# Seventeen token tiles turn their picks by a transposing DMA instead of on TensorE, with a new layout of the scattered buffer behind it

## The chip, the cores and the metric

The kernel runs on one core of one Trainium2 chip. The metric is device time in microseconds (us), from the launch of the program to its end. Five engines work side by side, each in its own fixed order: TensorE (PE; its weight loads are listed apart as PEld), VectorE (DVE), ScalarE (ACT), GpSimd (POOL) and SyncE (SP), whose only work here is to issue DMAs. An instruction whose input is not there yet holds up everything behind it on its engine.

## The reference, cut to what matters

Two layers, each a Fourier mixing followed by a product-key mixture of experts, with residuals. S = 2048 tokens, D = 512, H = 32 heads, E = 16 keys a side, 256 experts, and the best two of each side.

```
x = x + FNet(layernorm(x))        # y = Cr @ (x Wre') - Ci @ (x Wim'), C is 2048 x 2048
x = x + PEER(layernorm(x))        # and both once more, for the second layer

def PEER(x):                      # n tokens
    s1, s2 = q[..., :dk] @ k1.T, q[..., dk:] @ k2.T      # [n, 32 heads, 16] each
    i1, i2 = top 2 of s1, top 2 of s2                    # places, and values t1, t2
    cand   = t1[..., :, None] + t2[..., None, :]         # four sums of a head
    top_s, top_e = best 2 of cand, with e = 16 * i1 + i2
    g   = softmax(top_s)                                 # two weights of a head
    act = gelu(x @ u[top_e])
    out = sum over heads and picks of g * act * v[top_e]
```

## The kernel before

**Tiling.** The 2048 tokens are 16 tiles of 128. Each layer runs nine sequence units in the order `ORDER`: layer 0 takes units 0 to 8, layer 1 takes 0, 7, 1, 2, 3, 4, 5, 6, 8. Units 0 to 6 are 256 tokens (two tiles each), units 7 and 8 one tile each (tiles 14 and 15). The place of a unit in that order is called `at`. In a unit, `seq_unit` multiplies the whole layer-normed input (`xh` and `xl`, the high and low parts of fp32) with a block of the sequence DFT matrix. A block comes by DMA (`raw`, L454, four buffers), ACT takes its high part (`ch`, L458), DVE its low part (`cl`, L462), three buffers each, and PE runs three 128x512 matmuls for each of 64 pairs (L518). Then `ptl` and `pth` hold the result's parts (L544, L547).

**A token tile.** `token_tile` follows for each tile of the unit: the second DFT (L668), residual and layernorm (L682), the scores of all heads and keys (`pc`, L784 and L788), the scores of all experts (`xu`, L818), a long series of DVE steps that finds the best picks, and the matrix `q` of 3 x 128 columns a token (first place, second place and weight; each 2 x 2 x 32), written last by L985 and L1007. From there:

- PE turns `q` with three f16 transposes of 128x128 (`f_pq`, L1018), ACT copies the result out of PSUM (`f_qt`, L1022) as `qt`, with the heads' places reordered.
- DVE compares `qt` with a ramp into one-hot masks (`lr`, L1041, four a tile) and puts the weights on two of them (L1047, two a tile): "the masks".
- PE multiplies the masks in 32 small matmuls (L1057): "the blocks", two banks `pg`.
- ACT copies them to SBUF (L1089), two DMAs scatter them to DRAM (`gdr`, L1116), two read them back by token (`gt`, L1124), DVE multiplies them with the gelu (L1131), and either PE turns the product (L1162) and multiplies it with `v` (L1181, L1185), or, for the layer-1 tiles of `DEFERRED`, the product is stored (`ptd`, L1153) and multiplied at the end (`off`, L597).

**What sets the order.** All this is recorded as `Op`s with a duration, what they come after, which buffers (`Hold`) they take and give back, and a priority. `Plan.run` lays them out in time by these numbers, and the program is issued in the order of the planned starts. `lag` is the planned time from a DMA's issue to its landing, `shy` a further margin that its readers get, and `wary` a margin of 0.8 us (`WARY`) that PE operations of the middle stage get after inputs of other engines. Nothing of the plan waits at run time: an engine waits only for the semaphores of the data. The pools `q` (two buffers), `qt` (one), `lr` (four) and the eight lanes of DMAs in flight (`LANES`) bound what can overlap.

**Other moved work.** `MOVED` tiles (25 of 32) already turn their layernormed input over DRAM (`xdr`, L726; `tok`, L735, four DMAs) after a DVE transpose of 32x32 blocks, instead of on PE (L754).

Of the kernel before, what the change touches and what calls it, by code (L numbers as in the profile page):

```python
# [8 lines left out]
F32 = mybir.dt.float32  # L9
# [7 lines left out]
P = 128  # L17
# [7 lines left out]
SP = 1  # L25
# [15 lines left out]
    return at >= 2 if layer == 0 else at < NCH + NSC * (TPC - 1) - 2  # L41


def DEFERRED(layer, at):
    return layer == 1 and at < NCH + NSC * (TPC - 1) - 2


LATE = 13
STEP = 5 * E
ROW = 16 * STEP - E  # L50
WARY = 0.8
FILL0 = 10
FIRST = 4
# [14 lines left out]
class Op:  # L68
    def __init__(self, n, engine, us, fn, after, take, last, prio, lag, behind, shy):
        self.shy = shy  # L70
        self.n, self.engine, self.us, self.fn, self.prio, self.lag = n, engine, us, fn, prio, lag
        self.after, self.take, self.last, self.behind = after, take, last, behind
        self.start = self.end = None
        middle = len(prio) >= 4 and prio[0] == 0 and 3 <= NCH * prio[1] + prio[2] < 2 * NCH - 2 and prio[2] >= 0
        self.wary = WARY if engine == "PE" and middle else 0.0


# [85 lines left out]
def act(n):  # L163
    return 0.09 + n / 1.2e3
# [7 lines left out]
def spectral_peer_kernel(ctx: ExitStack, tc, x_in, cseq, ctile, dhid, wq, k1t, k2t, ut, vm, out):  # L172
# [7 lines left out]


    BUFS = {"acc": 4, "bank": 4, "raw": 4, "c": 3, "p": 1, "row": 4, "wr": 5, "wp": 2,
            "tok": 3, "sc": 1, "eq": 1, "act": 3, "q": 2, "top": 1, "qt": 1, "lr": 4, "gt": 1, "pp": 1, "gdr": 2, "xdr": 2, "bn": 1, "pick": 1}
    plan = Plan(BUFS)


# [423 lines left out]
    def token_tile(layer, n, i, t0, at):  # L610
# [408 lines left out]

        def f_qt():  # L1020
            t["qt"] = piece((3, P), dtype=F16) if fine else work([P, 3, P], F16, "qt")
            nc.scalar.copy(t["qt"].rearrange("p r (q j) -> p r q j", q=16),  # L1022
                           t["pq"].rearrange("p r (j q) -> p r q j", q=16))

        a = op("PE", 3 * TR16 + 0.06, f_pq, [c5, d2], take=[hb], last=[hq], prio=prio)
        a_qt = op("ACT", act(384), f_qt, [a], take=[hqt], last=[hb], prio=prio)

        def row_of(r, hf):
            m = t["qt"][:, r].rearrange("p (a b) -> p a b", b=4)[:, 16 * hf:16 * hf + 16]
# [22 lines left out]
        def f_blocks(hfs=(0, 1)):  # L1052
            for hf in hfs:
                pg = t["pg", hf] = bank([P, 8, E, 4])
                for g in range(8):
                    for j in range(2):
                        nc.tensor.matmul(pg[j * 64:(j + 1) * 64, g], t["m", hf, 0][:, 2 * g + j],  # L1057
                                         t["m", hf, 1][:, 2 * g + j], start=True, stop=True)

        def f_mask():  # L1060

# [48 lines left out]
        for hf in range(0 if fine else 2):  # L1110
            def f_out(hf=hf):
                if hf == 0:
                    t["gdr"] = dram.tile([2, E, 4, ROW], F32, name="gdr", bufs=BUFS["gdr"])
                d = t["gdr"][0]
                d = bass.AP(d.tensor, d.offset + hf * 8 * STEP, [[ROW, P], [STEP, 8], [1, 4 * E]])
                nc.sync.dma_start(d, t["gs", hf].rearrange("p g t e -> p g (t e)"))  # L1116
            moves.append(op("SP", 0.6, f_out, evac[hf:hf + 1], behind=moves[-1:], take=[] if hf else [hd], last=[hgs[hf]], prio=prio, lag=2.7))
        for j in range(0 if fine else 2):
            def f_in(j=j):
                if j == 0:  # L1120
                    t["gt"] = work([P, E, E], F32, "gt")
                d = t["gdr"][j]
                d = bass.AP(d.tensor, d.offset, [[STEP, 64], [4 * ROW, E], [1, E]])
                nc.sync.dma_start(t["gt"][j * 64:(j + 1) * 64], d)  # L1124
            back.append(op("SP", 0.6, f_in, moves, behind=back, take=[] if j else [hgt], last=[hd], prio=prio, lag=3.2, shy=0.5))
        if fine:
# [218 lines left out]
```

## Time and profile before

| what | value |
|---|---|
| median of 3 runs | 1234.31 us (1233.75 to 1234.34) |
| the profiled execution, its own time | 1233.48 us |
| its span in the trace | 1231.7 us |
| PE busy | 1220.1 us, 99% |
| DVE busy | 1000.1 us, 81% |
| ACT busy | 492.2 us, 40% |
| POOL busy | 45.0 us, 4% |
| DMA queue of SP, share of the 16 engines | 48.2% |
| granted TensorE clock | 1.00 |

Times are counted from the start of the span. Matmuls overlap in PE's pipeline: a 128x512 one is listed with some 0.39 us but the next starts about 0.23 us after it. What an instruction costs PE is therefore read from the starts of its neighbours, not from its own duration. Layer 0 fills roughly 7 to 660 us of the span (the preparation of the weights runs in its first 190 us, beside units 0 and on), layer 1 the rest. The page's columns are: line, engine, operation, output and inputs by the program's names, busy time, mean, and idle time before it with what ended it.

### The profile page before, as it was taken

How to read it: one execution, taken by the hardware profiler on the slowest of the kernel's cores; microseconds unless marked ns; L12 is line 12 of the kernel's file. 1: busy time of each engine (PE TensorE's matmuls, PEld its weight loads, DVE VectorE, ACT ScalarE, POOL GpSimd, SP SyncE). 2: the span in 40 equal slices, each digit the busy share in tenths (PEclk: the TensorE clock that was granted, in tenths of full speed). 3: DMA queues.
4: the chain of work that ended last, by engine and by line, in shares of the span. 5: the costliest groups of instructions: out<-in, count | busy, mean ns of one | idle time of the engine just before them, and what ended most of it. 6: DMA issues, size and time to landing. Idle time of an engine off the chain costs nothing. (4 is left out here: it accounts for less than half of the span.)

```text
span 1231.7 us, 20733 instructions
## 1 busy us (share of the span) xinstructions
PE 1220.1 (99%) x7626; PEld 1014.5 (82%) x7626; DVE 1000.1 (81%) x2272; ACT 492.2 (40%) x1010; POOL 45.0 (4%) x71
## 2 busy tenths in 40 slices
PE   9999999999999999999999999999999999999998
PEld 6877778878788888899988988788888888888886
DVE  8899997999897785968987359959596786859796
ACT  7522234334343333324654233334343333343455
POOL 2000000000000000000000000000000000000000
PEclk9999999999999999999999999999999999999999
DMA  7866551453444244441656243563635254454464
GB/s 241 261 200 218 188 169 35 101 119 83 123 122 113 70 116 116 107 120 49 172 142 174 79 120 82 125 135 92 154 97 140 73 145 111 99 141 104 115 204 144
DMA packets 312726, 160.12 MB, mean 130 GB/s; under 512 B 216752, under 2 KB 283056, under 8 KB 312624
## 3 DMA queue, kind: packets, MB, share of 16 engines
q1 hardware_dynamic: 312480, 158.66, 48.2%
q8 instruction: 60, 0.98, 0.3%
q14 instruction: 42, 0.34, 0.1%
q10 hardware_dynamic: 144, 0.13, 0.0%
HBM read 120.73 MB, written 38.01 MB: 129 GB/s over the span
## 5 line engine op out<-in xcount | busy, mean ns | idle before, releaser
L518 PE MATMUL acc<-ch,xh 128*128 128x512 f32 (+1 forms) x868 | 328.3, 378 | 0.8 <-DVE ptl L547 0.8
L518 PE MATMUL acc<-cl,xh 128*128 128x512 f32 (+1 forms) x868 | 321.9, 371 | 0.0
L518 PE MATMUL acc<-ch,xl 128*128 128x512 f32 (+1 forms) x868 | 321.7, 371 | 0.0
L458 ACT CAST ch<-raw 128x512 fp32r<-128x512 f32 x256 | 158.6, 620 | 272.0 <-PE acc L518 222.7
L462 DVE TENSOR_TENSOR cl<-raw,ch 128x512 fp32r<-128x512 f32 x256 | 176.0, 688 | 61.6 <-ACT ch L458 51.4
L518 PEld LDWEIGHTS acc<-cl,xh 128*128 128x128 f32 x868 | 163.6, 188 | 28.8
L518 PEld LDWEIGHTS acc<-ch,xh 128*128 128x128 f32 x868 | 163.6, 189 | 28.0 <-issue 1.8
L518 PEld LDWEIGHTS acc<-ch,xl 128*128 128x128 f32 x868 | 163.8, 189 | 25.6
L880 DVE TENSOR_TENSOR tmp<-sc 128x512 f32<-128x512 f32 (+1 forms) x64 | 43.5, 680 | 72.9 <-ACT sc L793 72.6
L784 PE MATMUL bank<-wh,tok 128*128 128x512 f32 x256 | 100.3, 392 | 0.3 <-ACT tok L742 0.3
L784 PE MATMUL bank<-wl,tok 128*128 128x512 f32 x256 | 99.7, 389 | 0.0
L668 PE MATMUL bank<-dh,pth 128*128 128x512 f32 x248 | 98.6, 397 | 0.0
L668 PE MATMUL bank<-dl,pth 128*128 128x512 f32 x248 | 96.7, 390 | 0.0
L668 PE MATMUL bank<-dh,ptl 128*128 128x512 f32 x248 | 93.6, 390 | 0.0
L793 ACT COPY sc<-bank 128x512 f32<-128x512 f32 x62 | 36.1, 588 | 138.1 <-PE bank L788 108.0
L1041 DVE TENSOR_TENSOR lr<-iota,qt 128x1024 f16<-128x1024 f16 x124 | 81.0, 686 | 12.0 <-ACT qt L1022 11.9
L260 POOL TENSOR_TENSOR stats<-stats,half 128x1 f32<-128x1 f32 x64 | 43.7, 689 | 1149.1 <-DVE stats L257 1135.1
L867 DVE TENSOR_TENSOR eq<-sc,val 128x1024 f16<-128x1024 f32 (+1 forms) x64 | 77.2, 1207 | 1.5
L518 PE MATMUL acc<-ch,xg 128*128 128x512 f32 (+1 forms) x204 | 77.3, 379 | 0.0
L518 PE MATMUL acc<-cl,xg 128*128 128x512 f32 (+1 forms) x204 | 75.7, 371 | 0.0
L518 PE MATMUL acc<-ch,xm 128*128 128x512 f32 (+1 forms) x204 | 75.7, 371 | 0.0
L788 PE MATMUL bank<-wh,tok 128*128 128x512 f32 x256 | 68.4, 389 | 0.0
(190 smaller groups left out, 2057.8 us busy)
## 6 DMA issues: line engine op xcount, KB each, us to landing
raw<-in_cseq SPq DMA_DIRECT2D x224, 256.0 KB, 2.8
wr<-in_wq SPq DMA_DIRECT2D x32, 512.0 KB, 3.8
gdr<-lr SPq DMA_DIRECT2D x62, 256.0 KB, 3.7
raw<-in_ctile SPq DMA_DIRECT2D x32, 256.0 KB, 2.9
xdr<-lr SPq DMA_DIRECT2D x25, 256.0 KB, 2.8
tok<-xdr SPq DMA_DIRECT2D x100, 64.0 KB, 2.6
wr<-in_x SPq DMA_DIRECT2D x16, 256.0 KB, 3.3
row<-in_x SPq DMA_DIRECT2D x16, 256.0 KB, 4.0
```

Of the source, the lines that this page charges most:

```text
L260: nc.gpsimd.tensor_tensor(st[:, 1:2], st[:, 1:2], half, op=ALU.pow)
L458: nc.scalar.copy(t[1], t[0])
L462: nc.vector.tensor_sub(t[2], t[0], as32(t[1]))
L518: nc.tensor.matmul(target(d), w[s][:, d * P:(d + 1) * P], moving(s % per, part), start=(s == 0 and k == 0 and d % blocks == 0), stop=(s == ...
L668: nc.tensor.matmul(t["y", cs.start], w[:, k, c, t0:t0 + P], r[:, c, k, cs], start=(not fine and z == 0 and c == 0 and m == 0), stop=(z == ...
L784: nc.tensor.matmul(t["pc", hf], t["th"][:, k, :], r[:, k, hf], start=(k == 0 and r is wh), stop=False)
L788: nc.tensor.matmul(t["pc", hf], t["tl"][:, k, :], wh[:, k, hf], start=False, stop=(k == KD - 1))
L793: nc.scalar.copy(t["sc"][:, :, hf, :], t["pc", hf].rearrange("p h e -> p e h"))
L867: nc.vector.tensor_tensor(t["eq"][:, :, cols], scores(), val(rank_, cols), op=ALU.is_equal)
L880: nc.vector.tensor_max(t["tmp"][:, :, cols], flat("sc")[:, :8, cols], flat("sc")[:, 8:, cols])
L1041: nc.vector.tensor_tensor(t["m", hf, r], io2, row_of(r, hf), op=ALU.is_equal)
```

## The change

`Q_MOVED` names 17 tiles: in layer 0 the places 2 to 4 (units 2, 3 and 4: tiles 4 to 9), in layer 1 the places 1 to 6 (units 7, 1, 2, 3, 4 and 5: tile 14 and tiles 2 to 11). For them the three transposes on PE and the copy on ACT are gone. SP stores `q` to DRAM (`qdr`, new line L1036) and loads it back with one transposing DMA of 384 x 128 f16 (L1040). The plan reckons 0.45 us and a lag of 2.0 us for the first, 1.2 us, a lag of 2.5 us and a margin (`shy`) of 2.0 us for the second. `qt` gets a second buffer.

[...] Last, `wary` begins at place 1 of layer 0 instead of place 3.

```
+def Q_MOVED(layer, at):
+    return ((2 <= at < 5) if layer == 0 else (1 <= at < 7))
-STEP = 5 * E
-ROW = 16 * STEP - E
+ROW = 68 * E
-        middle = len(prio) >= 4 and prio[0] == 0 and 3 <= NCH * prio[1] + prio[2] < 2 * NCH - 2 and prio[2] >= 0
+        middle = len(prio) >= 4 and prio[0] == 0 and 1 <= NCH * prio[1] + prio[2] < 2 * NCH - 2 and prio[2] >= 0
-    BUFS = {... "qt": 1, ...}
+    BUFS = {... "qt": 2, ... "qdr": 2, ...}
...
         def f_qt():
             t["qt"] = piece((3, P), dtype=F16) if fine else work([P, 3, P], F16, "qt")
-            nc.scalar.copy(t["qt"].rearrange("p r (q j) -> p r q j", q=16),
-                           t["pq"].rearrange("p r (j q) -> p r q j", q=16))
-        a = op("PE", 3 * TR16 + 0.06, f_pq, [c5, d2], take=[hb], last=[hq], prio=prio)
-        a_qt = op("ACT", act(384), f_qt, [a], take=[hqt], last=[hb], prio=prio)
+            if fine:
+                nc.scalar.copy(t["qt"].rearrange("p r (q j) -> p r q j", q=16),
+                               t["pq"].rearrange("p r (j q) -> p r q j", q=16))
+            else:
+                nc.scalar.copy(t["qt"], t["pq"])
+
+        if Q_MOVED(layer, at):
+            hqd = Hold("qdr")
+            def f_out():
+                t["qdr"] = dram.tile([3, P, P], F16, name="qdr", bufs=BUFS["qdr"])
+                nc.sync.dma_start(t["qdr"].rearrange("r t c -> t r c"), t["q"].rearrange("p r k a h -> p r (k a h)"))
+            def f_in():
+                t["qt"] = work([P, 3, P], F16, "qt")
+                nc.sync.dma_start(t["qt"].rearrange("p r t -> p (r t)"), t["qdr"].rearrange("r t c -> (r t) c"), transpose=True)
+            a = op("SP", 0.45, f_out, [c5, d2], take=[hqd], last=[hq], prio=prio, lag=2.0)
+            a_qt = op("SP", 1.2, f_in, [a], take=[hqt], last=[hqd], prio=prio, lag=2.5, shy=2.0)
+        else:
+            a = op("PE", 3 * TR16 + 0.06, f_pq, [c5, d2], take=[hb], last=[hq], prio=prio)
+            a_qt = op("ACT", act(384), f_qt, [a], take=[hqt], last=[hb], prio=prio)
...
-                        nc.tensor.matmul(pg[j * 64:(j + 1) * 64, g], t["m", hf, 0][:, 2 * g + j],
-                                         t["m", hf, 1][:, 2 * g + j], start=True, stop=True)
+                        half, n = (hf, 2 * g + j) if fine else (j, 8 * hf + g)
+                        nc.tensor.matmul(pg[j * 64:(j + 1) * 64, g], t["m", half, 0][:, n], t["m", half, 1][:, n], start=True, stop=True)
...
-                    t["gdr"] = dram.tile([2, E, 4, ROW], F32, name="gdr", bufs=BUFS["gdr"])
-                d = t["gdr"][0]
-                d = bass.AP(d.tensor, d.offset + hf * 8 * STEP, [[ROW, P], [STEP, 8], [1, 4 * E]])
+                    t["gdr"] = dram.tile([3 * E * 4 + 4, ROW], F32, name="gdr", bufs=BUFS["gdr"])
+                d = t["gdr"]
+                d = bass.AP(d.tensor, d.offset + hf * 32 * (ROW + E), [[ROW, P], [4 * (ROW + E), 8], [1, 4 * E]])
-            moves.append(op("SP", 0.6, f_out, ..., lag=2.7))
+            moves.append(op("SP", 0.6, f_out, ..., lag=3.1))
...
-                d = t["gdr"][j]
-                d = bass.AP(d.tensor, d.offset, [[STEP, 64], [4 * ROW, E], [1, E]])
+                d = t["gdr"]
+                d = bass.AP(d.tensor, d.offset + j * 64 * ROW, [[ROW + E, 64], [4 * ROW, E], [1, E]])
```

Since the plan is laid out anew, the order moves on every engine. Below it is shown for one moved tile, tile 9 of layer 0 (the second tile of unit 4, `at` 4). The line numbers of the changed program are 3 to 21 higher than those of the program before: L668 becomes L671, L547 L550, L462 L465, L985 and L1007 L988 and L1010, L1041 L1061, L1047 L1067, L1057 L1078, L1131 L1151.

On PE before, among the second DFT's matmuls of the same unit (`bank_5463`), the three transposes of tile 9's `q_5207` with their weight loads:

```order
L668 MATMUL bank_5463<-dh_100,pth_5386 128x512
L668 MATMUL bank_5463<-dl_101,pth_5386 128x512
L668 MATMUL bank_5463<-dh_100,ptl_5387 128x512
L1018 LDWEIGHTS q_5207
L1018 MATMUL bank_5473<-ident16_109,q_5207 128x128
L1018 LDWEIGHTS q_5207
L1018 MATMUL bank_5473<-ident16_109,q_5207 128x128
L1018 LDWEIGHTS q_5207
L1018 MATMUL bank_5473<-ident16_109,q_5207 128x128
L668 MATMUL bank_5463<-dh_100,pth_5386 128x512
L668 MATMUL bank_5463<-dl_101,pth_5386 128x512
L668 MATMUL bank_5463<-dh_100,ptl_5387 128x512
```

On PE now, the same unit's second DFT; tile 9's `q` is read nowhere on this engine:

```order
L671 MATMUL bank_5399<-dh_100,pth_5332 128x512
L671 MATMUL bank_5399<-dl_101,pth_5332 128x512
L671 MATMUL bank_5399<-dh_100,ptl_5333 128x512
L521 MATMUL acc_4751<-ch_5289,xg_83 128x512
L521 MATMUL acc_4751<-ch_5289,xm_99 128x512
L521 MATMUL acc_4751<-cl_5300,xg_83 128x512
```

Over the whole program 51 transposes and 51 weight loads are gone from PE, and nothing is added there.

On DVE before, tile 9 again: its last two writes of `q_5207`, one row of another tile, and the masks that read `qt_5483`:

```order
L985 TENSOR_TENSOR q_5207<-key_5208,df_5448 128x2x64
L1007 TENSOR_TENSOR q_5207<-gw_5454,q_5207 128x2x32
L1170 TENSOR_TENSOR pp_5470<-bank_5460,pp_5470 128x256
L1041 TENSOR_TENSOR lr_5485<-iota_110,qt_5483 128x1024
L1041 TENSOR_TENSOR lr_5487<-iota_110,qt_5483 128x1024
L1041 TENSOR_TENSOR lr_5496<-iota_110,qt_5483 128x1024
L1047 TENSOR_TENSOR lr_5487<-lr_5487,qt_5483 128x1024
```

On DVE now (`q_5198` and `qt_5447` are the same tile's):

```order
L988 TENSOR_TENSOR q_5198<-key_5199,df_5418 128x2x64
L1010 TENSOR_TENSOR q_5198<-gw_5420,q_5198 128x2x32
L550 TENSOR_TENSOR ptl_5333<-acc_4751,pth_5332 128x512
L465 TENSOR_TENSOR cl_5465<-raw_5257,ch_5456 128x512
L465 TENSOR_TENSOR cl_5470<-raw_5278,ch_5459 128x512
L550 TENSOR_TENSOR ptl_5333<-acc_4763,pth_5332 128x512
L1151 TENSOR_TENSOR act_5005<-act_5005,gt_5435 128x256
L1061 TENSOR_TENSOR lr_5492<-iota_110,qt_5447 128x1024
L1061 TENSOR_TENSOR lr_5505<-iota_110,qt_5447 128x1024
L1190 TENSOR_TENSOR pp_5503<-bank_5494,pp_5503 128x256
L1067 TENSOR_TENSOR lr_5505<-lr_5505,qt_5447 128x1024
```

Five rows of other work now stand between the last write of `q` and the first mask, where one stood; over the 17 tiles it is 5 to 20 rows now and 0 to 7 before.

On SP before, the queue in the same stretch; no DMA of `q` is in it:

```order
L1228 DMA x2d_120<-row_4591 128x512
L454 DMA raw_5528<-in_cseq 128x2x256
L1116 DMA gdr_5581<-lr_5579 128x8x64
L1116 DMA gdr_5581<-lr_5583 128x8x64
L1124 DMA gt_5616<-gdr_5581 64x16x16 x2
L454 DMA raw_5630<-in_cseq 128x2x256
```

On SP now (`gdr_5387` and `gt_5435` are tile 8's, one tile before):

```order
L1136 DMA gdr_5387<-lr_5376 128x8x64
L1136 DMA gdr_5387<-lr_5389 128x8x64
L1036 DMA qdr_5433<-q_5198 128x3x128
L1144 DMA gt_5435<-gdr_5387 64x16x16 x2
L1040 DMA_TRANSPOSE qt_5447<-qdr_5433 128x384
L457 DMA raw_5468<-in_cseq 128x2x256
L457 DMA raw_5483<-in_cseq 128x2x256
L1248 DMA x2d_120<-row_4422 128x512
```

The store of `q` and the transposing load stand on either side of tile 8's reading back, and two loads of the DFT matrix stand behind them.

More of the change, by code (lines that the diff above doesn't have):

```diff
@@ L182, in spectral_peer_kernel @@
     BUFS = {"acc": 4, "bank": 4, "raw": 4, "c": 3, "p": 1, "row": 4, "wr": 5, "wp": 2,
-            "tok": 3, "sc": 1, "eq": 1, "act": 3, "q": 2, "top": 1, "qt": 1, "lr": 4, "gt": 1, "pp": 1, "gdr": 2, "xdr": 2, "bn": 1, "pick": 1}
+            "tok": 3, "sc": 1, "eq": 1, "act": 3, "q": 2, "top": 1, "qt": 2, "lr": 4, "gt": 1, "pp": 1, "gdr": 2, "xdr": 2, "qdr": 2, "bn": 1, "pick": 1}
     plan = Plan(BUFS)
@@ L1112, in f_out @@
                 if hf == 0:
-                    t["gdr"] = dram.tile([2, E, 4, ROW], F32, name="gdr", bufs=BUFS["gdr"])
-                d = t["gdr"][0]
-                d = bass.AP(d.tensor, d.offset + hf * 8 * STEP, [[ROW, P], [STEP, 8], [1, 4 * E]])
+                    t["gdr"] = dram.tile([3 * E * 4 + 4, ROW], F32, name="gdr", bufs=BUFS["gdr"])
+                d = t["gdr"]
+                d = bass.AP(d.tensor, d.offset + hf * 32 * (ROW + E), [[ROW, P], [4 * (ROW + E), 8], [1, 4 * E]])
                 nc.sync.dma_start(d, t["gs", hf].rearrange("p g t e -> p g (t e)"))
-            moves.append(op("SP", 0.6, f_out, evac[hf:hf + 1], behind=moves[-1:], take=[] if hf else [hd], last=[hgs[hf]], prio=prio, lag=2.7))
+            moves.append(op("SP", 0.6, f_out, evac[hf:hf + 1], behind=moves[-1:], take=[] if hf else [hd], last=[hgs[hf]], prio=prio, lag=3.1))
         for j in range(0 if fine else 2):
```

## The prediction

> **What bounds the kernel now.** I read the page's busy lines first, then the stages, then PE alone row by row. The page:
>
> ```profile
> span 1231.7 us, 20733 instructions
> PE 1220.1 (99%) x7626; PEld 1014.5 (82%) x7626; DVE 1000.1 (81%) x2272; ACT 492.2 (40%) x1010; POOL 45.0 (4%) x71
> ```
>
> PE is the bound, and DVE has a fifth of the span to spare. The stages (length, then busy time of PE, PEld, DVE, ACT, POOL) show where PE still idles:
>
> ```profile
> 190.00:300.00 110.00, 108.66 (x640) 89.19 (x639) 100.96 (x252) 43.08 (x98) 3.81 (x5) 1.00 0.38 88
> 300.00:470.00 170.00, 169.12 (x953) 138.28 (x952) 140.94 (x344) 62.33 (x133) 8.51 (x12) 1.00 0.42 106
> 835.00:1145.00 310.00, 310.00 (x1693) 255.40 (x1692) 238.29 (x560) 117.02 (x247) 4.85 (x9) 1.00 0.47 116
> 1145.00:1232.00 87.00, 82.00 (x671) 71.44 (x669) 68.40 (x182) 45.60 (x103) 1.10 (x2) 0.99 0.55 160
> ```
>
> Between 835 and 1145 us, where ten of the seventeen changed tiles lie, PE idles 0.00 us: every slot taken off PE there shortens the run, and every wait put on PE lengthens it. The granted clock (third column from the end) is 1.00, and 0.99 in the last stage, so the clock takes no part.
>
> **The transposes (a gain).** What three of them cost PE is read from the starts of their neighbours. First the regular step, from the chain, then PE's timeline at the first and the last changed tile:
>
> ```profile
> 815.36 1.81 PE bank L784 x8
> ...
> 302.17 0.34 PE L1018 MATMUL bank<-ident,q 128*128 128x128 f16 x3
> 302.32 0.47 PE L518 MATMUL acc<-ch,xh 128*128 128x512 f32 x1
> 302.64 0.39 PE L518 MATMUL acc<-ch,xl 128*128 128x512 f32 x1
> ...
> 1142.58 0.34 PE L1018 MATMUL bank<-ident,q 128*128 128x128 f16 x3
> 1142.73 0.48 PE L668 MATMUL bank<-dh,pth 128*128 128x512 f32 x1
> 1143.04 0.39 PE L668 MATMUL bank<-dl,pth 128*128 128x512 f32 x1
> ```
>
> Eight matmuls in 1.81 us make a step of 0.227 us. The three transposes hold PE for 0.15 us (302.17 to 302.32), but the matmul behind them then takes 0.32 us until its successor starts, 0.09 more than a step. So the triple costs 302.64 - 302.17 - 0.227 = 0.24 us, and at 1142.58 as much. The same difference, taken at all 17 (with 0.12 us for the step where a 128x256 matmul follows), has a median of 0.245 us and a sum of 4.17 us. Nothing comes to PE in their stead (51 matmuls fewer, none more), and the blocks stay. Term: -4.17 us. By its busy time (mean 0.22 us each) the gain would look like 11 us; that counts the pipeline three times.
>
> [...]
>
> **ACT, PSUM, plain copy (nothing).** 17 copies of `qt` leave ACT, which is busy 40%, and the 14 plain copies that stay can only change there. 17 short holds of a PSUM bank go; where PE idles 0.00 us, a bank that comes free earlier buys nothing. Zero.
>
> **The margin `wary` from place 1 on (a gain).** Three stalls of PE lie in the two places that become wary (tile 2 twice, tile 4 once):
>
> ```profile
> 252.00 0.39 PE L518 MATMUL acc<-cl,xh 128*128 128x512 f32 x1
> 252.73 0.34 PE L1018 MATMUL bank<-ident,q 128*128 128x128 f16 x3 [0.35 <-DVE q L985]
> ...
> 272.34 0.39 PE L518 MATMUL acc<-cl,xg 128*128 128x512 f32 x1
> 273.03 0.44 PE L1162 MATMUL bank<-identf,act 128*128 128x128 f32 x2 [0.30 <-DVE act L1131]
> ...
> 321.44 0.39 PE L518 MATMUL acc<-cl,xh 128*128 128x512 f32 x1
> 322.70 0.44 PE L1162 MATMUL bank<-identf,act 128*128 128x128 f32 x2 [0.88 <-DVE act L1131]
> ```
>
> Start to start less one step, they cost 0.50, 0.46 and 1.03 us. A margin of 0.8 us takes the first two and 0.8 of the third: 1.76 us. The new order agrees: counted in steps, PE has 0.7 us more work ahead of tile 2's transposes, and between blocks and L1162 2.7 us more for tile 2 and 2.1 for tile 4. Bounds 0 (the plan slips elsewhere) and 1.99 (all three); I take 1.76.
>
> **The way over DRAM (a possible loss).** Of such a transposing load the trace has no row. Its way is: last write of `q`, store, load, first mask. The nearest DMAs (count, KB each, median us from issue to landing):
>
> ```profile
> x2d<-row SPq DMA_DIRECT2D x16, 256.0 KB, 2.0
> gdr<-lr SPq DMA_DIRECT2D x62, 256.0 KB, 3.7
> tok<-xdr SPq DMA_DIRECT2D x100, 64.0 KB, 2.6
> wr<-in_dhid SPq DMA_DIRECT2D x4, 512.0 KB, 4.5
> gt<-gdr SPq DMA_DIRECT2D x62, 64.0 KB, 3.0
> ```
>
> The store (96 KB in pieces of 256 bytes) lies between 2.0 and 3.7 us; the load (96 KB) between 2.6 and 4.5 us, if a transposing one is like some plain one. Together 4.6 to 8.2 us; I take 6.5, above the middle, since the pieces are small as in `gdr`, and since for tile 9 the load stands behind tile 8's reading back, which itself waits for `gdr` (3.7 us).
>
> What the order allows is read for tile 9, one of the two tightest. Before, on DVE and PE:
>
> ```profile
> 450.19 0.23 DVE L1007 TENSOR_TENSOR q<-gw,q 128x64 f16<-128x64 f32 x1 [0.37 <-ACT q L1006]
> ...
> 452.32 1.90 DVE L1041 TENSOR_TENSOR lr<-iota,qt 128x1024 f16<-128x1024 f16 x3 [1.26 <-ACT qt L1022]
> ...
> 456.54 0.67 DVE L1047 TENSOR_TENSOR lr<-lr,qt 128x1024 f16<-128x1024 f16 x1
> ...
> 458.64 0.69 PE L1057 MATMUL bank<-lr 128*64 128x64 f16 x32
> ```
>
> From the last write of `q` (450.42) to the first mask took 1.90 us, and the masks were done (457.21) 1.43 us ahead of the blocks, of which 0.4 us is the least that this hop took in any changed tile (tile 5). From tile 9's scores to its blocks the order now has 18 more matmuls and six transposes fewer: 18 x 0.227 - 6 x 0.05 = 3.8 us more of PE's work. So the way may take 1.9 + 3.8 + 1.0 = 6.7 us before PE waits. The same working gives 6.7 us for tile 11 of layer 1, 7.6 for its tile 5, 8.2 for its tile 10, and 9.4 to 22 us for twelve others. Only for tile 5 of layer 0 it gives nothing, since its blocks moved up 3.2 us: there other DVE work left the way (20 rows stand between `q` and masks now). At 6.5 us no tile waits; at 8.2 us three do, by 1.5, 1.5 and 0.6: 3.6 us. Bounds 0 and 3.6; I take 0.5, as some tile will be late.
>
> **The SP queue.** The load waits there for the store's landing, up to 3.7 us, with loads of the DFT matrix (`raw`) behind it. Those have cover (who waited for what: us in total, times, longest):
>
> ```profile
> SPq L454 <- DVE cl L462: 320.4, 129, 15.0
> ...
> ACT ch L458 <- DMA raw<-in_cseq: 5.7, 4, 2.7
> ...
> DVE act L1131 <- DMA gt<-gdr: 1.9, 2, 1.3
> ```
>
> SP spends 320 us waiting for a free `raw` buffer, and ACT waits only 5.7 us in all for one to land. Four buffers at one block in 12 steps (2.7 us) are 10.9 us ahead. 34 DMAs of 96 KB add 3.3 MB to 160. Zero; if the cover were gone, a late `ch` would be next. SP's issue itself has no row and no reader beside these.
>
> **The layout of `gdr`.** Number and size of the pieces stay, the distances change; what that does to 3.7 and 3.0 us no row shows. It lies between a few tenths less and, taking the 4.5 us row as the worst, 0.8 + 1.5 us more. Before, DVE waited for `gt` twice in all, 1.9 us (last row above), so most of it is hidden; and in PE's order the work between blocks and L1162 is 1.3 to 2.7 us more than before for tiles 1 to 5, and from 1.4 less to 2.0 more for the rest of layer 0. Zero, with the upper end in the range.
>
> **The end.** After 1155 us the chain runs through DVE for some 30 us, starting behind the scores of the last pair of tiles:
>
> ```profile
> 1154.71 0.60 ACT sc L793
> ```
>
> Those scores come earlier as PE does, so the gain passes on, unless tile 11's masks, 2.4 us later against PE's work, push this DVE stretch: bounds 0 and +2.4, taken 0, since its blocks stand ahead of that stretch.
>
> **The sum**, against the profiled execution (1233.48 us, span 1231.7): -4.17 - 1.76 + 0.5 = -5.43, so 1228.05. That execution was 0.83 us below the median 1234.31; on the median's footing 1228.9 us.
>
> **Rivals.**
>
> A. *Only the transposes pay, and a part is given back at the end.* The new order stalls PE in other places as much as the three stalls did (term 0 instead of -1.76), and tile 11 pushes the DVE stretch by 2.4 us: 1234.31 - 4.17 + 2.4 = 1232.5, within 0.2%. For it: the end is already DVE's. Against: the transposes alone make 1230.1, and the margin acts just where the stalls are.
>
> B. *The masks come late and PE waits (slower).* If the way takes longer than the order allows, DVE stands at the mask with `cl` behind it, PE at the blocks, and each changed tile pays anew. At 9.3 us tile 9 pays 2.6, tile 11 2.6, tile 5 of layer 1 1.7 and tile 10 1.1: 8.0 us, so 1228.4 (no 0.5) + 8.0 = 1236.4; about there it turns from no change to slower (over 1236.8). At 12 us ten tiles pay 27 us, and the time passes 1250. For it: the transposing load is the one operation here without a row. Against: 9.3 us is 1.1 above the worst pair of plain DMAs.
> [...]
>
> C. *Loads of `raw` fall behind the waiting SP.* One late `ch` costs up to the 2.7 us seen; two or three such make 1234 to 1236, no change. Against: the waits quoted above.
>
> **How the numbers follow.** About 0.2% (2.5 us) is what a measurement of this kernel tells from no change. The forecast has 0.60, and milder forms of A that still end below 1231.8 have 0.04: faster 0.64. A has 0.12 and C 0.07: no change 0.19. B has 0.17: slower. The time is the forecast's, 1228.9. Low end: 1234.31 - 4.17 - 1.99 = 1228.1, and 0.8 for small waits that a new order may also take away, 1227.3. High end: 1237.0, just past B's turning point; beyond it lies somewhat over 0.1.
>
> **What would show it.** PE's matmuls 7575 instead of 7626, its busy time some 4 us lower, and idle time in 190 to 300 us down from 1.34 us towards 0.5. The transposing load's landing: below 4.5 us confirms the way, above 6 brings B. A wait of DVE's mask for `qt<-qdr` with several us in all, and of PE's blocks behind it, would be B's mark; ACT's `ch` waiting for `raw` well over 5.7 us C's; and 835 to 1145 us is where any such wait shows as idle PE. A load that lands late, or takes all 16 DMA engines for long, would make the prediction wrong.

## The result, and the profile after

The changed kernel takes 1226.32 us (median of 6 runs, 1225.76 to 1227.04), the one before 1234.32 us (1233.69 to 1234.88). The ratio is 0.9936, with a 95% interval of 0.9923 to 0.9948: 8.0 us less. Forecast were 5.4 us less, and 1226.32 lies 1 us below the low end of the range, 1227.3. The profiled execution of the changed kernel took 1226.32 us too, with a span of 1224.5 us; the one of before had 1233.48 and 1231.7. So 7.2 of the 8.0 us can be looked for in the two traces, and the remaining 0.8 us is that the profiled execution of before lay below its median.

Page of the changed kernel:

```profile
span 1224.5 us, 20672 instructions
PE 1216.2 (99%) x7575; PEld 1013.4 (83%) x7575; DVE 999.3 (82%) x2272; ACT 483.0 (39%) x993; POOL 48.9 (4%) x71
```

7575 matmuls and 3.9 us less of busy PE, as foreseen. The stages of the changed kernel (length, then busy time of PE, PEld, DVE, ACT and POOL, granted clock, DMA share, GB/s):

```profile
190.00:300.00 110.00, 110.00 (x642) 90.46 (x642) 99.29 (x247) 41.81 (x96) 3.64 (x5) 1.00 0.34 87
300.00:470.00 170.00, 170.00 (x953) 140.31 (x952) 141.10 (x350) 60.68 (x131) 10.62 (x12) 1.00 0.47 118
835.00:1145.00 310.00, 309.88 (x1670) 255.84 (x1669) 236.65 (x545) 110.18 (x228) 6.17 (x10) 1.00 0.48 121
1145.00:1232.00 87.00, 74.84 (x636) 65.40 (x634) 63.30 (x170) 44.23 (x100) 0.55 (x1) 0.98 0.55 159
```

In the first two stages PE idled 1.34 and 0.88 us before; now it idles 0.00 in both. Between 835 and 1145 us, where ten tiles go over DRAM, 0.12 us of idle time has come. The last row counts 7.2 us less of PE because the run ends that much earlier. The transfers of the changed kernel (count, KB each, median us from issue to landing):

```profile
gdr<-lr SPq DMA_DIRECT2D x62, 256.0 KB, 2.9
tok<-xdr SPq DMA_DIRECT2D x100, 64.0 KB, 2.6
gt<-gdr SPq DMA_DIRECT2D x62, 64.0 KB, 3.0
qdr<-q SPq DMA_DIRECT2D x17, 96.0 KB, 1.8
qt<-qdr SPq DMA_TRANSPOSE x17, 2.4
```

The store of `q` lands after 1.8 us and the transposing load after 2.4 us. Both are below the lower bounds that the rows of before gave (2.0 and 2.6). What the one tile shown in the prediction makes of it, tile 9 of layer 0, on DVE, SP and PE of the changed kernel:

```profile
443.13 0.23 DVE L1010 TENSOR_TENSOR q<-gw,q 128x64 f16<-128x64 f32 x1
443.38 0.38 SPq L1036 DMA_DIRECT2D qdr<-q  x1
445.26 1.28 SPq L1040 DMA_TRANSPOSE qt<-qdr  x1
449.40 1.28 DVE L1061 TENSOR_TENSOR lr<-iota,qt 128x1024 f16<-128x1024 f16 x2
...
454.85 0.68 DVE L1067 TENSOR_TENSOR lr<-lr,qt 128x1024 f16<-128x1024 f16 x1
...
457.11 0.69 PE L1078 MATMUL bank<-lr 128*64 128x64 f16 x32
```

The last write of `q` ends at 443.36; SP issues the load (445.26) once the store has landed, 1.8 us after its issue, and its landing is recorded at 448.2. That makes a way of 4.85 us. DVE is at other work then and comes to the masks 1.2 us later; the masks are done 1.6 us ahead of the blocks. In all 17 tiles the way has a median of 4.7 us, 4.1 to 4.9 us in fourteen of them and 8.1 us in the slowest (tile 14 of layer 1, whose store stood 2 us in SP's queue and took 3.7 us to land). The waits of the changed kernel (who waited for what: us in total, times, longest):

```profile
ACT tok L745 <- DMA tok<-xdr: 7.2, 5, 2.1
ACT ch L461 <- DMA raw<-in_cseq: 5.6, 3, 2.1
...
DVE act L1151 <- DMA gt<-gdr: 4.7, 2, 4.3
...
DVE lr L1061 <- DMA qt<-qdr: 1.4, 1, 1.4
```

Of 17 tiles one mask waited for its load, 1.4 us (the slow one). ACT's wait for `raw` is as it was. What grew is ACT's wait for `tok`, from 1.4 to 7.2 us, and DVE's for `gt`, from 1.9 to 4.7.

**Where the 7.2 us are.** I took every matmul's start-to-start time less the step of its form (0.227 us for 128x512 and so on; own working over all of PE's rows). What is left over falls into the short groups with the slower matmul behind them, and into stalls of over 0.13 us:

| us | before | after | difference |
|---|---|---|---|
| triples of `q` and the slower matmul behind each | 7.68 | 4.00 | -3.68 |
| stalls 190 to 590 us | 2.88 | 0.00 | -2.88 |
| stalls 590 to 670 us | 0.49 | 0.87 | +0.38 |
| stalls 670 to 1145 us | 0.99 | 0.75 | -0.24 |
| stalls from 1145 us on | 1.50 | 0.89 | -0.61 |
| everything else | | | -0.14 |
| span | 1231.71 | 1224.54 | -7.17 |

So the triples brought about half, and the stalls 3.35 us, where the prediction had 1.76 - 0.5 = 1.26. 2.88 of the stalls went between 190 and 590 us; the three named ones are 1.99 of that. The fourth was at the blocks of tile 0. PE before:

```profile
219.82 0.44 PE L1057 MATMUL bank<-lr 128*64 128x64 f16 x16
220.95 0.44 PE L1057 MATMUL bank<-lr 128*64 128x64 f16 x16 [0.69 <-ACT lr L1089]
```

And PE after, the same blocks:

```profile
219.31 0.69 PE L1078 MATMUL bank<-lr 128*64 128x64 f16 x32
```

The second sixteen of the 32 blocks waited for ACT's copy of the first sixteen: in the program before, both halves of tile 0 lie in the same PSUM bank, and in no other tile do they. After the change they have two, and all 32 run in one go. This is worth 0.86 us (start to start), and it was not in my sum. Which banks the halves get changes with other edits of the program too: in the kernel with the new layout alone (below), whose order is that of before, they have two. So this gain is an accident of the new program and not the work of the moves.

### The profile page after: what moved, and what is told of

Read it like the earlier page. It is cut to its first block, busy times and chain, and to the rows that moved or that the text cites. A ratio compares the mean times of both kernels' runs of the same rounds, so it can differ in the third digit from the quotient of the medians.

```text
span 1224.5 us, 20672 instructions
## 1 busy us (share of the span) xinstructions
PE 1216.2 (99%) x7575; PEld 1013.4 (83%) x7575; DVE 999.3 (82%) x2272; ACT 483.0 (39%) x993; POOL 48.9 (4%) x71
## 4 chain that ended last, share of the span: by engine, by line
PE 93%; DVE 4%; DMA 1%; SPq 0%; ACT 0%; issue 0%; POOL 0%; ACTq 0%; DVEq 0%; POOLq 0%
PE acc L521 52%; PE bank L671 12%; PE bank L787 9%; PE bank L791 5%; PE bank L821 3%; PE bank L521 2%; PE bank L1078 2%; PE acc L600 2%; PE bank L1201 1%; PE bank L395 1%; DVE w L387 1%; DVE w L384 1%; PE bank L1205 1%; PE acc L501 1%; PE acc L671 1%; DMA wr<-in_wq 1%
## 5 line engine op out<-in xcount | busy, mean ns | idle before, releaser
L465 DVE TENSOR_TENSOR cl<-raw,ch 128x512 fp32r<-128x512 f32 x256 | 175.3, 686 | 60.6 <-ACT ch L461 44.9
L671 PE MATMUL bank<-dh,pth 128*128 128x512 f32 x248 | 98.0, 395 | 0.5 <-ACT pth L547 0.5
L671 PE MATMUL bank<-dl,pth 128*128 128x512 f32 x248 | 96.6, 390 | 0.0
L671 PE MATMUL bank<-dh,ptl 128*128 128x512 f32 x248 | 93.6, 391 | 0.0
L263 POOL TENSOR_TENSOR stats<-stats,half 128x1 f32<-128x1 f32 x64 | 47.6, 748 | 1138.3 <-DVE stats L260 1064.8
L1061 DVE TENSOR_TENSOR lr<-iota,qt 128x1024 f16<-128x1024 f16 x124 | 80.7, 683 | 2.1 <-DMA qt<-qdr 1.4
```

The lines of the kernel that those rows point to most:

```text
L263: nc.gpsimd.tensor_tensor(st[:, 1:2], st[:, 1:2], half, op=ALU.pow)
L465: nc.vector.tensor_sub(t[2], t[0], as32(t[1]))
L671: nc.tensor.matmul(t["y", cs.start], w[:, k, c, t0:t0 + P], r[:, c, k, cs], start=(not fine and z == 0 and c == 0 and m == 0), stop=(z == ...
L1061: nc.vector.tensor_tensor(t["m", hf, r], io2, row_of(r, hf), op=ALU.is_equal)
```

## Experiments

Each of them is compared with the kernel before, run on the same chip; its medians there were 1234.1 to 1234.2 us. "Stalls" are the stalls of PE after 190 us, by the working above; before has 5.86 us of them, after 2.51. Where the text says "triples", the slower matmul behind each is counted with them.

**The new layout of `gdr` alone** (the kernel before, with the plain copy, the new pairing of the blocks and the new distances; the order of instructions is the same on every engine). The plain copy leaves the heads' places in `qt` as they are in `q`, as the transposing load does, so the blocks pair other columns of the masks and their results stand elsewhere in `gdr`. There are still two stores of 8 pieces of 256 bytes a partition, with the rows of neighbouring partitions 4352 bytes apart instead of 5056, and two loads of 16 pieces of 64 bytes a token, with neighbouring tokens 4416 bytes apart instead of 320.

```
-STEP = 5 * E
-ROW = 16 * STEP - E
+ROW = 68 * E
...
+                        half, n = (hf, 2 * g + j) if fine else (j, 8 * hf + g)
...
+                d = bass.AP(d.tensor, d.offset + hf * 32 * (ROW + E), [[ROW, P], [4 * (ROW + E), 8], [1, 4 * E]])
```

> The kernel before with the new layout of gdr alone (plain copy of qt, other pairing of the masks, other distances); the planned numbers and so the order of every engine stay as before. In the result the stores of gdr landed after 2.9 us instead of 3.7. Theory S (the gain is PE's slots, 17 x 0.245 us, and the stalls that the margin wary takes away): the layout pays nothing by itself, 1234.3 within 0.5 us, and the stalls of PE at L1162 (0.46 us for tile 2, 1.03 us for tile 4) stay. Theory L (the faster stores took the stalls away): gt is read 0.8 us earlier, both stalls go, 1.3 us less, 1233.0.

Measured: 1232.47 us (1231.84 to 1232.97), ratio 0.9986 (0.9977 to 0.9995). The scattered store lands after 3.0 us instead of 3.7, but the stalls that wait for its reading back stayed as long as they were. PE of this kernel:

```profile
272.16 0.44 PE L1164 MATMUL bank<-identf,act 128*128 128x128 f32 x2 [0.30 <-DVE act L1133]
...
321.81 0.44 PE L1164 MATMUL bank<-identf,act 128*128 128x128 f32 x2 [0.85 <-DVE act L1133]
```

0.30 and 0.88 us before, 0.30 and 0.85 now. So the faster store takes none of the three stalls away. Laid beside before, matmul by matmul, the profiled execution gains 0.86 us at tile 0's blocks, which here have two banks, and 0.29 us at 602 us, and little more until the end (1.2 us in all). The median fell by 1.8 us where no change was expected: 0.86 us of that is the banks, and the rest is not traced to a cause. Nothing that waits for the stores or their reading back got shorter by more than 0.03 us at the two stalls, so zero for the layout's own transfers stands.

**The margin alone** (the kernel before with one line):

```
-        middle = ... and 3 <= NCH * prio[1] + prio[2] < 2 * NCH - 2 and prio[2] >= 0
+        middle = ... and 1 <= NCH * prio[1] + prio[2] < 2 * NCH - 2 and prio[2] >= 0
```

> The kernel before with wary from place 1 of layer 0 on, nothing else. Theory S: the three stalls of tiles 2 and 4 go (1.76 us), 1232.5. Theory L: only the one at tile 2's transposes, which no store stands before, goes: 0.5 us, 1233.8. Theory P (any new plan draws its stalls anew, by chance): between 1232 and 1236, with other stalls in other places.

Measured: 1232.27 us (1231.36 to 1233.79), ratio 0.9986 (0.9977 to 0.9994). The three stalls are gone, and tile 0's too, but a new one of 0.93 us has come in the same stretch, PE of this kernel:

```profile
380.21 0.34 PE L1018 MATMUL bank<-ident,q 128*128 128x128 f16 x3 [0.76 <-DVE stats L257]
```

and 0.57 us near the end. Stalls are 4.63 us, 1.23 less than in before, although the three and tile 0's bank were 2.85: the margin does what it says where it says it, and more than half of the sum comes back elsewhere. The 1.97 us less of the median agree with theory S's 1.76 in part by accident, since tile 0's bank is in them and the new stalls are too.

**The moved tiles without the margin** (the changed kernel with that line put back):

> The changed kernel with wary from place 3 again. Theory S: the stalls at places 1 and 2 come back, up to 1.8 us, 1228.1. Theory L: 1226.3 to 1226.8, the faster stores still cover them. Theory P: 1225 to 1230, with stalls in new places.

Measured: 1230.06 us (1229.24 to 1230.30), ratio 0.9966 (0.9953 to 0.9978). Triples 3.84 us, near the changed kernel's 4.00. Stalls are 5.58 us. Of the three that the margin was to take, only the first is back, smaller (0.35 us start to start), and the largest stall is new; PE of this kernel:

```profile
251.72 0.34 PE L1021 MATMUL bank<-ident,q 128*128 128x128 f16 x3 [0.19 <-DVE q L988]
...
600.39 0.50 PE L671 MATMUL bank<-dh,pth 128*128 128x512 f32 x1 [1.84 <-ACT pth L547]
```

The row at 600.39 is the second DFT waiting for its input, in a place with no moved tile; it costs 2.0 of the 5.58 us. Theory S gave 1228.1 with all three stalls back; two stayed away without the margin. So the new order can take them as well as the margin can, and which of the two took them in the changed kernel is not separated.

**The margin and the layout without the moves** (the changed kernel with `Q_MOVED` returning False):

> The changed kernel with no tile moved (the layout, the margin wary, the lag of 3.1 us and two buffers of qt stay): the 17 triples are back on PE. Theory S: 17 x 0.245 = 4.2 us more than the changed kernel, 1230.5, and the profile's triples sum to 32 again. Theory P: anywhere from 1229 to 1234, by the stalls of its plan.

Measured: 1230.55 us (1230.33 to 1231.02), ratio 0.9971 (0.9960 to 0.9982), as expected. From here to the changed kernel the 17 moves bring 4.2 us. Triples 7.56 against 4.00 us: 3.6 us, or 0.21 us each. The two traces differ by 4.7 us, and the rest is that this plan has 1.1 us more of stalls; so the 4.2 us agree with 17 x 0.245 in part by luck. Between 190 and 590 us this kernel has 1.03 us of stalls, the margin alone 0.93: the planned landing of 3.1 us and the second buffer of `qt`, which both stay here, do not empty that stretch either.

**What a transpose costs PE** (the kernel before, with every triple but the last tile's done twice, 93 transposes more):

```
-            for r in range(3):
+            for r in [0, 1, 2] * (1 if fine else 2):
```

> The kernel before, with the three transposes of q issued twice in a row in every tile but the last (31 tiles, 93 more matmuls of the same data into the same bank); the order is otherwise as before, and the plan doesn't know of them. Theory S (0.056 us a step inside a group, 0.09 us once for the change back to fp32 matmuls): 93 x 0.056 = 5.2 us more, less the 0.9 us that tile 0's blocks waited in the kernel before and don't in this program (their two banks lie apart): 1238.5. Rival G (a triple costs 0.245 us wherever it stands): 31 x 0.245 - 0.9 = 6.7 us more, 1240. Rival R (the busy time of 0.22 us a transpose is what it costs): 20 us more, 1254.

Measured: 1237.96 us (1235.97 to 1239.88), ratio 1.0030 (1.0018 to 1.0042). PE of this kernel:

```profile
302.06 0.51 PE L1018 MATMUL bank<-ident,q 128*128 128x128 f16 x6
302.37 0.48 PE L518 MATMUL acc<-ch,xh 128*128 128x512 f32 x1
302.69 0.40 PE L518 MATMUL acc<-ch,xl 128*128 128x512 f32 x1
```

Six hold PE 0.31 us (three held it 0.15), and the matmul behind them takes 0.32 us until its successor, as behind three. Over all of them the 93 more cost 5.36 us, 0.058 each, and the slower matmul behind costs the same as before, about 0.09 a group. So the price read from the starts, 0.15 + 0.09 a triple, is the right one, and neither the busy time (0.22 us each) nor the same price per triple wherever it stands (rival G, 1240 us) is. What the 0.09 us come from is not shown. It is not the change from f16 back to fp32 that theory S named, since the matmul behind a pair of fp32 transposes is as slow. PE of the kernel before:

```profile
322.89 0.47 PE L518 MATMUL acc<-ch,xh 128*128 128x512 f32 x1
323.21 0.39 PE L518 MATMUL acc<-ch,xl 128*128 128x512 f32 x1
```

These stand behind the two transposes L1162 at 322.70 us and step 0.32 us; behind all 19 such pairs that a 128x512 matmul follows the median is 0.314 us, as behind the 27 triples that one follows.

**A longer way** (the changed kernel, with `q` copied twice from DRAM to DRAM between store and load; the plan does not know of it):

```
+                for n in range(2):
+                    far = dram.tile([3, P, P], F16, name=f"far{n}", bufs=BUFS["qdr"])
+                    nc.sync.dma_start(far, t["qdr"])
+                    t["qdr"] = far
```

> The changed kernel with the way over DRAM made longer: q goes through two more DRAM buffers (two copies of 96 KB, each waiting for the one before) ahead of the transposing load; the planned order stays. In the changed kernel's trace the way took 4.1 to 4.9 us in 14 of 17 tiles and the first mask began 1.2 to 6.5 us after the landing in all tiles but one. Theory W (PE pays what the way exceeds the order's allowance): some 4.4 us more of way, paid by six or so tiles with 9 us in all, 1235. Rival H (the allowance is far larger or refilled elsewhere): 1226.5. Rival Q (SP stands longer in its queue, the DFT blocks come late): well over 1240, with ACT waiting for raw.

Measured: 1249.11 us (1247.51 to 1251.09), ratio 1.0122 (1.0108 to 1.0135); the way is 8.7 to 13.0 us. Waits of this kernel:

```profile
DVE lr L1065 <- DMA qt<-far: 21.1, 12, 6.2
ACT tok L745 <- DMA tok<-xdr: 20.7, 7, 6.0
PE bank L1082 <- DVE lr L1071: 10.7, 6, 3.0
...
ACT ch L461 <- DMA raw<-in_cseq: 6.0, 4, 2.3
```

Twelve masks wait, and PE behind them, while `raw` is no later than before. This is rival B with the mechanism that it named, but both prices were too low: the expectation by some 14 us, and rival B's working, which gave 8 us for a way of 9.3 us, the median here. Stalls are 26.6 us, 24.1 more than in the changed kernel. A part is told by PE's timeline behind one of these waits:

```profile
813.76 1.02 PE L1082 MATMUL bank<-lr 128*64 128x64 f16 x31 [2.96 <-DVE lr L1071]
...
816.16 0.63 PE L521 MATMUL acc<-ch,xh 128*128 128x512 f32 x1
816.58 0.63 PE L521 MATMUL acc<-ch,xl 128*128 128x512 f32 x1
```

and by the stretches around it, of the same kernel (columns as in the stages above, granted clock third from the end):

```profile
810.00:813.70 3.70, 0.68 (x2) 0.40 (x3) 3.11 (x6) 0.62 (x1) 0.00 (x0) 0.90 0.72 207
813.70:820.00 6.30, 6.24 (x44) 5.08 (x44) 1.30 (x3) 1.60 (x3) 0.00 (x0) 0.52 0.92 232
820.00:826.00 6.00, 6.00 (x34) 5.16 (x33) 1.11 (x2) 1.50 (x3) 0.00 (x0) 1.00 0.52 67
```

After the wait the matmuls step 0.427 us instead of 0.227 for some 5 us; the granted clock of the stretch from 813.70 to 820 us is 0.52. There are 33 such steps after 190 us in this kernel (one in before, one in the changed kernel), 6.6 of the 24.1 us. The other 17.5 us are waits, 10.7 of them blocks waiting for late masks (the third row above). How the rest divides is not separated: SP also has the two copies in its queue, which land after 2.3 and 2.2 us, and ACT waits 20.7 us for `tok` against 7.2 in the changed kernel.

**No margin for the load's landing** (the changed kernel, `shy=0.0` for the transposing load in place of 2.0):

> The changed kernel with the margin (shy) of the transposing load at 0 instead of 2.0 us: masks are planned up to 2 us earlier. Theory S (the margin is not what the gain rests on; the plan without it still reckons 6.2 us for a way of some 4.5): 1226.3 within 1 us. Rival M (the margin keeps PE from waiting): 1228 to 1231, with waits of DVE for qt<-qdr of several us. Theory P (a new plan draws new stalls): up to 2 us either way without such waits.

Measured: 1230.33 us (1229.47 to 1231.50), ratio 0.9969 (0.9956 to 0.9981). The masks hardly wait for the load, as the waits of this kernel show:

```profile
DVE lr L1061 <- DMA qt<-qdr: 1.0, 2, 0.7
```

Yet stalls are 7.26 us, 3.09 of them between 590 and 670 us, where no tile is moved; of the moved tiles' blocks only those of tile 14 of layer 1 waited for their masks, 0.56 us. So most of the 4.0 us lost are not waits for the load. The time is rival M's, its mechanism (several us of masks waiting) is not there; new stalls of a new plan, as in theory P, are, though twice as large as it allowed.

**Twenty-five tiles** (the changed kernel with more tiles moved):

```
-    return ((2 <= at < 5) if layer == 0 else (1 <= at < 7))
+    return ((1 <= at < 7) if layer == 0 else (at < 7))
```

> The changed kernel with 25 tiles moved instead of 17 (layer 0 places 1 to 6, layer 1 places 0 to 6). Theory S: eight more triples off PE, 8 x 0.245 = 2.0 us less, 1224.3. Theory P: the new plan's stalls add or take up to 2 us. Rival B: the tiles at the layer's edges are needed soon, PE waits there, 1227 to 1230.

Measured: 1229.90 us (1229.82 to 1231.60), ratio 0.9967 (0.9954 to 0.9979). The triples fall further, to 2.41 us with a wait of 0.5 us inside one group, but stalls rise to 9.0 us, 4.0 of them between 590 and 670 us, and ACT waits 14.4 us for `tok`:

```profile
ACT tok L745 <- DMA tok<-xdr: 14.4, 6, 3.7
```

So eight triples more bring no gain: the time is rival B's (1227 to 1230), 3.6 us above the changed kernel. Between 190 and 590 us this kernel has 1.7 us of stalls, although it has the moves and both margins.

**Plans a little beside it.** By then the triples were settled and the stalls were not: every new order had others. So four kernels that differ from before or after in one number of the plan alone, in no computation: the load's margin 1.7 and 2.3 in place of 2.0, the margin `WARY` 1.0 in place of 0.8, and the kernel before with 2.8 for 2.7 us of landing in the store of `gdr`.

```
-... hqd], prio=prio, lag=2.5, shy=2.0)      # after
+... hqd], prio=prio, lag=2.5, shy=1.7)      # and, in another kernel, shy=2.3
...
-WARY = 0.8                                  # after
+WARY = 1.0
...
-... last=[hgs[hf]], prio=prio, lag=2.7))    # before
+... last=[hgs[hf]], prio=prio, lag=2.8))
```

> The changed kernel with a margin of 1.7 us instead of 2.0 on the transposing load, a small nudge of the plan. Theory D (draw: whatever isn't the triples is the sum of PE's stalls, which each new order draws anew, between 2.5 and 8 us in the kernels so far, most of it at the end of layer 0): 1226 to 1231, with the time following the stalls at 1218.1 + 4.0 + stalls in the span. Theory M (the margin itself takes stalls away): about 1226.9, 0.15 of the way to the 1230.3 of no margin.

> The changed kernel with a margin of 2.3 us. Theory D: 1226 to 1231, no order by the margin. Theory M: 1226.0 to 1226.3, no more stalls than with 2.0.

> The changed kernel with the margin wary at 1.0 us instead of 0.8 for the PE operations of the middle stage. Theory M (margins remove stalls, more margin removes more): stalls between 590 and 1145 us fall below the 1.6 us of the changed kernel, 1225.0 or less. Theory D: 1226 to 1231.

> The kernel before with a planned lag of 2.8 instead of 2.7 us for the stores of gdr, a small nudge of its plan. As in the kernel before, and unlike all the experiments so far, the two banks of tile 0's blocks are one and the same PSUM bank in this program. Theory K (that shared bank is what stalls PE in the middle of tile 0's blocks): a stall of 0.86 us at some 221 us stands in this profile too. Theory D: 1232 to 1236 in time by the other stalls. If the faster stores or the pairing had taken that stall away in the layout experiment: it stands here too, but then it should also have stood with wary alone, where it didn't.

| kernel | median us | ratio, 95% | triples | stalls 190 to 590 | stalls from 590 on |
|---|---|---|---|---|---|
| before | 1234.32 | | 7.68 | 2.88 | 2.98 |
| before, 2.8 for 2.7 | 1231.84 (1231.28 to 1232.59) | 0.9980 (0.9971 to 0.9989) | 7.60 | 2.82 | 1.54 |
| after | 1226.32 | 0.9936 (0.9923 to 0.9948) | 4.00 | 0.00 | 2.51 |
| after, load's margin 1.7 | 1227.46 (1226.86 to 1228.21) | 0.9947 (0.9932 to 0.9962) | 3.82 | 0.00 | 4.61 |
| after, load's margin 2.3 | 1227.51 (1226.61 to 1228.40) | 0.9947 (0.9932 to 0.9962) | 3.54 | 0.00 | 3.74 |
| after, `WARY` 1.0 | 1234.83 (1233.42 to 1237.63) | 1.0006 (0.9997 to 1.0016) | 3.55 | 0.00 | 4.51 |

What stays the same within each kind: the triples, and the stretch from 190 to 590 us. That stretch in one row (PE's busy time stands behind the length), in the kernel before:

```profile
190.00:590.00 400.00, 397.79 (x2370) 332.83 (x2369) 332.16 (x803) 149.47 (x321) 16.05 (x23) 1.00 0.40 99
```

with the margin alone:

```profile
190.00:590.00 400.00, 399.24 (x2388) 334.62 (x2387) 332.39 (x808) 147.48 (x322) 17.42 (x23) 1.00 0.41 99
```

with the moves, without the margin:

```profile
190.00:590.00 400.00, 399.50 (x2379) 335.59 (x2378) 334.21 (x806) 146.56 (x317) 15.88 (x23) 1.00 0.41 103
```

and in the changed kernel:

```profile
190.00:590.00 400.00, 400.00 (x2391) 336.84 (x2391) 333.24 (x812) 146.26 (x317) 18.43 (x23) 1.00 0.41 103
```

PE idles 2.2 us there in before (and in its neighbour), 0.8 with the margin alone, 0.5 with the moves alone, and nothing with both, in all four plans that have the 17 moves, both margins and 1.7 us or more for the load. With 25 moves, with no margin for the load or with the long way it is not empty (1.7, 1.9 and 5.7 us of stalls). Tile 0's wait for its bank is in the neighbour of before as well, and in no other kernel of this study; PE of that neighbour:

```profile
220.16 0.44 PE L1057 MATMUL bank<-lr 128*64 128x64 f16 x16
221.29 0.44 PE L1057 MATMUL bank<-lr 128*64 128x64 f16 x16 [0.69 <-ACT lr L1089]
```

This is theory K: the bank, and not the stores or the pairing, made that wait. What does not stay: the stalls from 590 us on, 1.5 to 3.0 us in the two plans of before and 2.5 to 4.6 us in the four of after. Theory M fails, since neither a larger margin for the load nor a larger `WARY` lowered them. Theory D's 1226 to 1231 holds for the two margins and not for `WARY` 1.0: that kernel is 8.5 us slower than the changed one although its stalls are only 2.0 us more. Its page has a group that neither before nor after has (count, busy us, mean ns, idle time before):

```profile
L1311 PE MATMUL acc<-dh 128*128 128x512 f32 x27 | 6.6, 394 | 0.0
```

These 27 matmuls compute nothing that is used. The program puts them on PE where the plan has a hole of over 1 us near the end, and they run from 1220.6 us on, with the last reading back of `gt` issued at 1220.1 and 1221.6 beside them. 27 steps of 0.227 are 6.1 us: this plan has left no work over to lay beside the last way through DRAM. So one number beside the change can take back all that it brings.

None of these kernels is faster than the changed one. Of the four plans of after in the table it is the fastest by 1.1 us, so a part of its 8.0 us is luck of the plan.

## Why the prediction was right or wrong

- **The transposes, -4.17 us: right in kind and nearly in size.** Measured 3.68 us in the profile against before, and 3.6 us against the kernel without the moves. The six transposes confirm both parts of the price.
- **ACT, PSUM, the plain copy, 0: this step failed in part.** The copies and the triples' holds of a bank brought nothing seen, but the new program gave tile 0's two halves two banks and so took away 0.86 us. The trace of before had the row of that wait; I asked only what the triples' banks do. That the wait went is an accident of the new program: with the layout alone and with the margin alone it went too.
- **The margin and the way, -1.76 + 0.5 = -1.26 us: this term was mis-sized, and it carried the time out of the range.** The profile has -3.35. Piece by piece the difference of 2.09 us is: 0.50 us allowed for a late tile that cost nothing seen, 0.23 us since the third stall went whole, 0.86 us for the bank, and 0.50 us net elsewhere. That the margin can take the three stalls is shown (margin alone: all gone), and that moves and margin together empty the stretch from 190 to 590 us is shown by the neighbours. But the moves without the margin left only 0.35 us of the three, so how much of the 1.76 us is the margin's own is not shown. The net 0.50 us is not a term but luck: the three plans beside the changed kernel are 1.1, 1.2 and 8.5 us slower.
- **The way over DRAM: taken as 6.5 us, measured 4.7.** The store and the load are each below the lower bound from plain DMAs. One tile was late, tile 14 of layer 1, which is none of the four that the prediction named as tight: its store stood in SP's queue. Its masks waited 1.4 us, and PE did not pay for it here; in the two plans with 1.7 and 2.3 us its blocks waited 0.54 and 0.71 us. So 0.5 was a fair size for a late tile, and that it cost nothing is luck of this plan. The transposing load, which had no row before, landed after 2.4 us (2.3 to 2.9 over the 17 tiles), and the 9.3 us from which rival B was worked out did not come. The median way of 4.7 us stays 2.0 us below the 6.7 us that the prediction gave the two tightest tiles.
- **The SP queue, 0: right for `raw`, too narrow.** `raw` waits 5.6 us against 5.7, so rival C is out. I named only `raw` behind the waiting load. `tok` became later, 7.2 against 1.4 us of ACT's waiting. PE paid for it once, and it had paid once before the change too. PE before, then PE of the changed kernel:

```profile
601.97 0.50 PE L784 MATMUL bank<-wh,tok 128*128 128x512 f32 x1 [0.34 <-ACT tok L742]
```

```profile
804.23 0.49 PE L787 MATMUL bank<-wh,tok 128*128 128x512 f32 x1 [0.30 <-ACT tok L745]
```

  That is 0.49 us before and 0.47 us after, so the later `tok` cost PE nothing more. Whether the transposing loads make it later stays open: the margin alone, without any, has 7.0 us of that wait, the 25 tiles 14.4, the long way 20.7.
- **The layout of `gdr`, 0: right.** The store got faster, not slower (3.7 to 2.9 us), and the two stalls behind it stayed when the layout was put in alone.
- **The end, 0: right.** Stalls from 1145 us on are 0.6 us less, and the gain passed on.
- **The rivals.** A asked for stalls elsewhere as large as the three, and a later end; the changed kernel has neither, but its neighbour with `WARY` 1.0 shows how it would look, with 6.1 us at the end. B did not happen here since the way is short; its mechanism is real, and it costs more than its working said (22.8 us by medians where the way has a median of 9.3 us), in part since PE's matmuls took 0.427 us a step in place of 0.227 after some of its waits.
- **The range.** Its low end took the three stalls and 0.8 us more. All stalls of before after 190 us are 5.86 us, and a plan laid out anew can lose any of them: the neighbour of before, with one number changed, is 2.3 us faster than it on the same chip, 1.5 us of it stalls. A low end some 2 us lower would have said so. The footing of 0.83 us between profiled execution and median, carried over to the changed kernel, did not hold for it either, and is a third of the miss of 2.6 us.

## What to carry to other kernels

Where PE is full, price a removed PE instruction by its neighbours' starts, and test that price by doubling the instruction. Where a planner lays everything out anew, list every stall of the bounding engine in the profile, not only those that the change aims at, and set the range from what two or three neighbouring plans do; a single result can sit some microseconds beside its neighbours (here 1.1, 1.2 and 8.5 us). The way through DRAM, hidden behind other work, cost PE nothing seen here at a median of 4.7 us; made 4.6 us longer it cost 22.8 us, since waits spread and some were followed by steps of 0.427 us.

## What the runs showed of the hardware

- **About half speed after some waits of PE.** In the kernel with the long way PE's waits of 2.96, 1.74 and 2.46 us before the blocks at 813.76, 1030.04 and 1096.80 us were followed by matmuls at 0.427 us a step in place of 0.227, behind the second one after 0.8 us. Behind the first there are ten such steps in a row, and the granted clock from 813.70 to 820 us is 0.52. A single wait of 1.84 us, in the kernel with the moves but without the margin `wary`, was not followed by them: its matmuls step 0.23 us from the second on, and the granted clock from 600.30 to 606 us is 1.00. What sets the two cases apart is not shown.
- **The transposing load was about as quick as plain loads.** 384x128 f16 values (96 KB) land 2.4 us (2.3 to 2.9) after the issue began, of which SP's issue holds 1.1 to 1.3 us in all tiles but one (1.8); plain loads of 64 KB (`tok`) have 2.6 us.
- **The distances of a scattered store mattered.** Number and size of the pieces were kept, and the store of 256 KB went from 3.7 to 2.9 us (3.0 with the layout alone). With the old distances the margin alone has 3.6 us; with the new ones the long way has 2.9 us, the moves without the margin 3.0, the margin and the layout without the moves 3.1, and `WARY` 1.0 3.2.
- **Two PSUM tiles that follow one another shared a bank, and the order of instructions did not tell it.** The kernel with the new layout alone has the order of before. Where the two halves of tile 0's blocks had one bank (before and its neighbour with 2.8 us), the second sixteen waited for ACT's copy of the first, 0.69 us of idle PE; where they had two, all 32 ran in one go.
